# Seven block products of the gated experts: first differences and a second block kept in PSUM, two products of the next unit drawn ahead, weight sums split later

## The chip, the cores and the metric

One core of a Trainium2 chip runs the whole program. The metric is the device time in microseconds (us), median of three runs. TensorE (PE in the profile, PEld its weight loads), VectorE (DVE), ScalarE (ACT), GpSimd (POOL) and the DMA queues work side by side, each in its own program order, and wait for each other through semaphores. SP only issues DMAs.

## The reference, cut to what matters

Attention with a bias, then a dense layer with softplus, then eight experts whose outputs are weighted by a gate that is normalised over tokens and experts. The change lies in the last part alone:

```
N, D, E, F = (1152, 512, 8, 1024)
P = np.exp(logits)            # then 8 rounds of row and column normalisation
for e in range(E):
    h = np.maximum(x @ w1[e], 0.0)
    ye = h @ w2[e]
    out += P[:, e:e + 1] * ye
```

Everything is fp32. Each operand of a matmul is split into a high part (rounded) and a low part (the rest), and a product is three matmuls: high by high, low weights by high, high weights by low.

## The kernel before, in words

**Units.** The two feed-forward stages are cut into 40 units of 256 hidden columns: units 0 to 7 are the dense layer, and each expert has four. Units 12 to 39 (experts 1 to 7) are "gated": their hidden values are multiplied by the gate `pb` right after the ReLU. Units 12 to 38 are "fast" and are the subject here. Of 1152 tokens, 1024 go through blocked products and the last 128 through plain ones (`up_last`, `turn_last`, `last_sum`).

**Seven products in place of eight.** Tokens and hidden columns are split in two by two blocks, and both matrix products of a unit are done with seven block products (Strassen, Winograd's form) instead of eight. In the text P1 to P7 are the up products (x by w1, six matmuls each, 128x512 out), and D1 to D7 the down products (h by w2, six matmuls each). The blocks of h are B11, B12, B21, B22; their sums are T1 = B12 - B11, T2 = B22 - T1, T3 = B22 - B12, T4 = B21 - T2. D1 takes B11, D5 takes T1, D6 takes T2, D3 B22, D7 T3, D2 B21, D4 T4. "First" of a block is ACT's rounded copy (high part), "second" the subtraction that gives the low part, on DVE or POOL.

**PSUM.** Chains `X`, `Y`, `Z` are running sums: P1, P6, P7, P4 add into bank `t`, P2 sits in `tail`, P5 and P3 in `pv`. The four `sum` banks take the down products.

**Order of a fast unit on PE before.** P2, P6, P5, P7, P3, the plain product of the last tokens (in bank `tail`), P4, then P1 of the next unit, then D1, two transposes, D5, D6, `last_sum`, D3, D7, D2, D4. `after` runs what follows each product: copies of the running sum to SBUF on ACT (`keep`: v1 after P1, u2 after P6, u3 after P5), and for P2, P7, P3, P4 an addition (`add`) and `weighted`, one DVE instruction max(x, 0) * pb that gives B22, B11, B12, B21, followed by the differences and splits. Before, B11 and T1 are in SBUF: `u3` and a half of `fs[2]`.

**Weights.** `load` brings w1 into `fs[0]` and w2 into `fs[3]` by SP's DMAs. `mix` (POOL, four instructions) writes the sums of the w1 blocks to `fs[1]`, `mixd` (POOL, four) those of w2 to `fs[4]`. `high` and `highd` split w1 (`wu`) and w2 (`wd`), `highs` the sums in `fs[4]` (tiles `raw` for the high part, `room` for the low part). In gated units a split by `parts` is two ACT instructions of 128x1024, high = src and low = -src, and a DMA issued by POOL that adds src to low. `DOWN_JOBS` says after which down product of a unit each of these is issued.

**Entry.** At unit 12 the gate's columns come from DRAM (`shares_of(1)` for `pb`, `publish` for expert 0), and the sum of expert 0 so far is multiplied by them (`weigh_columns`).

Of the kernel before, what the change touches and what calls it, by code (L numbers as in the profile page):

```python
# [11 lines left out]
F32R = mybir.dt.float32r  # L12
# [101 lines left out]
def attention_moe_moe_kernel(ctx: ExitStack, tc, qT, kT, vN, wpos, w_in, w_out, w_gate, e_w1, e_w2,  # L114
# [503 lines left out]
    def experts(m0, accp, xr):  # L618
# [107 lines left out]

        def parts(w, src, by_dma=False):
            hi, lo = (w[:, 0], w[:, 1]) if not isinstance(w, tuple) else w
            nc.scalar.activation(hi, src, AF.Copy)  # L729
# [23 lines left out]
        def highs(u, k):  # L753
            if fast(u):
                if not wss:
                    wss.extend([again(3, [128, 1024], F32R), pool["spare"][:, 0:1024]])
                parts(tuple(wss), fs[4], True)

# [103 lines left out]

        full = {}

        def weighted(u, n, src):
            name = {2: "B22", 7: "B11", 3: "B12", 4: "B21"}[n]
            extra = [fs[2][:, 512 * k:512 * k + 512] for k in range(2)]
            full[name] = hold["u3"] if n == 4 and fast(u) else extra[0] if n == 4 else hold[{2: "v1", 7: "u3", 3: "u2"}[n]]
            c = int(n in (7, 4))
            if fast(u) and n == 3:  # L870
                full.update(T1=extra[0], T2=extra[1], T3=full["B12"])
            elif fast(u) and n == 4:
                full["T4"] = extra[1]
            t = h[name] = pool["moe"].tile([128, 2, 512], F32R, tag="h", bufs=4, name="h")
            nc.vector.scalar_tensor_tensor(out=full[name], in0=src, scalar=0.0, in1=pb[c], op0=ALU.max, op1=ALU.mult)  # L875
            if not fast(u):
                first(name)
                h[c, int(n in (7, 3))] = t
                lows.append(lambda: second(nc.vector, name))
            elif n == 2:  # L880
                held.append(lambda: first(name))
            elif n == 7:
                first(name)
                second(nc.gpsimd, "B22")
            elif n == 3:
# [4 lines left out]
                first("T1")  # L890
                first("T2")
                second(nc.vector, "T1")
                second(nc.gpsimd, "T2")
                difference(nc.gpsimd, "T3", "B22", "B12")
            else:
                h["T4"] = tss[2]
                first(name)

        def soften(u, c, f):
# [50 lines left out]
        def up_last(u):  # L950
            zr, n, xl = bank("t" if u < U1 and u in PLAIN else "tail"), 0, pool["xl"]
            for k in range(KT):
# [15 lines left out]
        def down_fast(u):  # L968
            product(u + 1, 1)
            begun.add((u + 1, 1))  # L970
            banks = {x: ps2("sum") for x in "XZ"}
            for at, (n, x, a, b, (c, i)) in enumerate(DOWN):
# [3 lines left out]
                for k, f in order:  # L976
                    wo, ho = ((0, 0), (1, 0), (0, 1))[k]
                    nc.tensor.matmul(banks[x][:, f], ws[wo][:, o + 128 * f:o + 128 * f + 128], h[b][:, ho],  # L978
                                     start=(n in (1, 5, 2) and k == 0), stop=(k == 2), skip_group_check=True)
                for fs_ in (slice(0, 2),) if at else (slice(0, 1), slice(1, 2)):  # L980
                    d = acc[c][:, 2 * i:2 * i + 2][:, fs_]
                    nc.vector.tensor_tensor(out=d, in0=banks[x][:, fs_], in1=d, op=ALU.add)  # L982
                if at == 0:
                    turn_last(u)
                    difference(nc.gpsimd, "T4", "B21", "T2")
                    first("T3")
                    second(nc.gpsimd, "T3")
                    if u > U1 + UE:
                        weights["high"](u + 1, 1)
                    first("T4")  # L990
                    second(nc.gpsimd, "B21")
                    second(nc.gpsimd, "T4")
                if at == 3:
                    after(u + 1, 1)
                if at == 2:
                    r = last_sum(u, "pv")
                if at == 6:
                    evac(u, 2, 0, r)
                for what, ahead, k in DOWN_JOBS.get(at, ()):
# [5 lines left out]

        def weigh_columns(c, i):
            d = acc[c][:, 2 * i:2 * i + 2]
            nc.vector.tensor_tensor(
                out=d, in0=d, in1=pb["first"][:, 512 * c:512 * c + 512].rearrange("p (o n) -> p o n", o=1).to_broadcast([128, 2, 512]),
                op=ALU.mult)  # L1010
# [203 lines left out]
        def publish():  # L1214
# [112 lines left out]
        def unit(u):  # L1327
# [87 lines left out]
            ask(u, "r2")  # L1415
            if gated(u) and (u + 1 - U1) % UE == 0 and u + 1 < NU:
                shares_of((u + 1 - U1) // UE)
            load_up()
# [212 lines left out]
```

## Time and profile before

| what | value |
|---|---|
| median of 3 runs | 1238.3 us (1238.29 to 1239.51) |
| the profiled execution: its own time, its span | 1237.1 us, 1235.3 us |
| busy of the span: PE, DVE, POOL, ACT | 94%, 77%, 68%, 59% |
| P2 of unit 13 to P2 of unit 14 | 22.77 us |
| P2 of unit 14 to P2 of unit 39, 25 units | 610.73 us |

All times are us from the start of the span. A row of a timeline is: start, duration, engine, line, operation, output and inputs, sizes, how many merged, and in brackets the idle time of the engine before it and what ended that. A row of the windows view is: the stretch, its length, the busy time of PE, PEld, DVE, ACT and POOL with their instructions, the granted TensorE clock as a share of full speed, the busy share of the DMA engines and GB/s. A row of instruction groups ends with the busy time, the mean of one in ns, and the idle time before them.

### The profile page before, as it was taken

How to read it: one execution, taken by the hardware profiler on the slowest of the kernel's cores; microseconds unless marked ns; L12 is line 12 of the kernel's file. 1: busy time of each engine (PE TensorE's matmuls, PEld its weight loads, DVE VectorE, ACT ScalarE, POOL GpSimd, SP SyncE). 2: the span in 40 equal slices, each digit the busy share in tenths (PEclk: the TensorE clock that was granted, in tenths of full speed). 3: DMA queues.
4: the chain of work that ended last, by engine and by line, in shares of the span. 5: the costliest groups of instructions: out<-in, count | busy, mean ns of one | idle time of the engine just before them, and what ended most of it. 6: DMA issues, size and time to landing. Idle time of an engine off the chain costs nothing.

```text
span 1235.3 us, 19730 instructions
## 1 busy us (share of the span) xinstructions
PE 1166.2 (94%) x7289; PEld 959.0 (78%) x7289; DVE 952.2 (77%) x1472; ACT 727.3 (59%) x1190; POOL 835.7 (68%) x854
## 2 busy tenths in 40 slices
PE   5989999999999999989999999999999999999998
PEld 5888999888888878768777777777777777777777
DVE  9976988498888665658778877878777878777874
ACT  7976887775455553345654565566556555654552
POOL 8236777567878853336777777678767876777770
PEclk9999999999999999989999999999999999999999
DMA  5769663033223211074566566655666567557552
GB/s 137 229 172 249 205 199 90 1 104 102 78 94 102 69 34 35 1 182 92 120 138 151 122 137 132 149 121 127 143 136 130 121 144 162 114 121 159 136 103 94
DMA packets 82568, 152.41 MB, mean 123 GB/s; under 512 B 9312, under 2 KB 47016, under 8 KB 82472
## 3 DMA queue, kind: packets, MB, share of 16 engines
q0 software_dynamic: 15984, 58.20, 25.4%
q1 hardware_dynamic: 66056, 92.51, 24.7%
q8 instruction: 57, 0.93, 0.3%
q10 hardware_dynamic: 432, 0.45, 0.1%
q14 instruction: 39, 0.32, 0.1%
HBM read 78.79 MB, written 14.14 MB: 75 GB/s over the span
## 4 chain that ended last, share of the span: by engine, by line
PE 68%; DVE 20%; DMA 4%; ACT 3%; issue 3%; POOL 1%; SPq 1%; DVEq 0%; ACTq 0%; POOLq 0%
PE sum L978 18%; PE t L815 10%; PE sum L1044 10%; DVE u L875 9%; PE pv L815 5%; PE op L544 5%; PE pv L1060 4%; PE tail L815 4%; DVE f L861 3%; PE sps L453 3%; PE tp L503 2%; DVE u L838 2%; PE tail L954 1%; DVE pv L838 1%; PE t L833 1%
## 5 line engine op out<-in xcount | busy, mean ns | idle before, releaser
L982 DVE TENSOR_TENSOR acc<-sum,acc 128x512 f32<-128x512 f32 (+1 forms) x216 | 232.8, 1088 | 68.8 <-PE sum L978 60.1
L815 PE MATMUL t<-room,wu 128*128 128x512 f32 x592 | 161.1, 391 | 1.0 <-ACT u L843 0.5
L858 POOL TENSOR_TENSOR raw<-f,raw 128x512 fp32r<-128x512 f32 x54 | 77.3, 1431 | 124.5 <-ACT raw L854 124.5
L854 ACT ACTIVATE h<-u 128x512 fp32r<-128x512 f32 x83 | 52.5, 633 | 177.7 <-DVE u L875 146.0
L1044 PE MATMUL sum<-h,wd 128*128 128x512 f32 x576 | 138.7, 394 | 0.0
L815 PEld LDWEIGHTS t<-room,wu 128*128 128x128 f32 x592 | 110.3, 188 | 26.1 <-ACT u L843 1.4
L1044 PEld LDWEIGHTS sum<-h,wd 128*128 128x128 f32 x576 | 105.4, 188 | 22.2 <-DVE acc L1081 0.9
L815 PE MATMUL pv<-x,wu 128*128 128x512 f32 x444 | 114.8, 394 | 5.9 <-ACT u L843 5.8
L978 PE MATMUL sum<-h,wd 128*128 128x512 f32 x324 | 93.8, 413 | 26.2 <-DVE h L858 26.0
L729 ACT ACTIVATE wu<-f 128x1024 fp32r<-128x1024 f32 x77 | 81.0, 1052 | 41.1 <-POOL f L725 23.6
L815 PEld LDWEIGHTS pv<-x,wu 128*128 128x128 f32 x444 | 83.8, 190 | 24.3 <-ACT u L843 6.7
L978 PEld LDWEIGHTS sum<-h,wd 128*128 128x128 f32 x324 | 56.8, 188 | 57.1 <-DVE h L858 36.5
L875 DVE SCALAR_TENSOR_TENSOR u<-u,pb 128x512 f32<-128x512 f32 x28 | 91.2, 3256 | 1.0
L815 PE MATMUL t<-x,wu 128*128 128x512 f32 x296 | 85.5, 390 | 0.0
L838 DVE TENSOR_TENSOR u<-t,u 128x512 f32<-128x512 f32 x37 | 25.6, 691 | 75.9 <-PE t L815 73.6
L854 ACT ACTIVATE raw<-f 128x512 fp32r<-128x512 f32 x81 | 50.7, 626 | 55.8 <-DVE f L861 55.2
L269 PE MATMUL pac<-bw,m 128*128 128x64 bf16 (+1 forms) x1920 | 66.8, 198 | 17.3 <-DVE bw L241 12.0
L269 PEld LDWEIGHTS <-m 128*128 128x128 bf16 (+1 forms) x1920 | 63.1, 105 | 20.9 <-issue 9.6
L734 POOL TENSOR_TENSOR wu<-f,wu 128x1024 fp32r<-128x1024 f32 x21 | 53.0, 2523 | 38.1 <-ACT wu L729 37.4
L858 POOL TENSOR_TENSOR h<-u,h 128x512 fp32r<-128x512 f32 x54 | 77.9, 1443 | 0.0
L732 POOL DMA_DIRECT2D wu<-f x56 | 49.6, 886 | 39.8 <-ACT wu L731 23.4
L1081 DVE TENSOR_TENSOR acc<-sum,acc 128x512 f32<-128x512 f32 x80 | 55.1, 688 | 24.7 <-PE sum L1044 24.0
(296 smaller groups left out, 3168.8 us busy)
## 6 DMA issues: line engine op xcount, KB each, us to landing
f<-in_e_w_dram SPq DMA_DIRECT2D x128, 256.0 KB, 4.0
wu<-f POOLq DMA_DIRECT2D x56, 512.0 KB, 4.6
wd<-f POOLq DMA_DIRECT2D x28, 512.0 KB, 6.7
room<-f POOLq DMA_DIRECT2D x27, 512.0 KB, 7.5
raw<-in_w_in_dram SPq DMA_DIRECT2D x16, 512.0 KB, 3.6
raw<-in_w_out_dram SPq DMA_DIRECT2D x16, 512.0 KB, 3.4
bias<-wt SPq DMA_DIRECT2D x14, 576.0 KB, 5.4
raw<-in_qT_dram SPq DMA_DIRECT2D x16, 288.0 KB, 5.4
```

What stands on the lines that cost most here:

```text
L269: nc.tensor.matmul(pt[0:n, g], lhs, win(w, (k * (ng + 1) + gw) * NC, [[(ng - gw) * NC, 2], [1, NC]]), start=(k == 0), stop=(k == 2))
L544: nc.tensor.matmul(op[:, 0:n], l, r, start=(part == 0 and k == 0), stop=(part == 8))
L729: nc.scalar.activation(hi, src, AF.Copy)
L815: nc.tensor.matmul(zz, wu(u)[:, a, o:o + 128], xs[xn][b][j], start=(n in (1, 2, 5) and k == 0), stop=(k == 5), skip_group_check=True)
L838: nc.vector.tensor_tensor(out=out, in0=hold[bank_], in1=hold[name], op=ALU.add)
L854: nc.scalar.activation(h[name][:, 0], full[name], AF.Copy)
L858: eng.tensor_tensor(out=t[:, 1], in0=full[name], in1=t[:, 0].bitcast(F32), op=ALU.subtract)
L875: nc.vector.scalar_tensor_tensor(out=full[name], in0=src, scalar=0.0, in1=pb[c], op0=ALU.max, op1=ALU.mult)
L978: nc.tensor.matmul(banks[x][:, f], ws[wo][:, o + 128 * f:o + 128 * f + 128], h[b][:, ho], start=(n in (1, 5, 2) and k == 0), stop=(k == 2) ...
L982: nc.vector.tensor_tensor(out=d, in0=banks[x][:, fs_], in1=d, op=ALU.add)
L1044: nc.tensor.matmul(s, lhs, rhs, start=(n == 0), stop=(n == 5))
L1081: nc.vector.tensor_tensor(out=d, in0=o, in1=d, op=ALU.add)
```

## The change

Four things in fast units. B11 is written to the PSUM bank that P2 used (`tail`) and T1 to that of P5 and P3 (`pv`); T2 and T4 share one half of `fs[2]`. The plain product of the last tokens goes to the `sum` bank `Z`, and the splits of T1 and T2 and the difference T3 move behind it (`split_t`). B21 is computed after D1 instead of after P4. P2 of the next unit is drawn ahead into the down products, between D7 and D2. The split of the w2 sums moves from the down products (both ACT instructions and the DMA after D2) into the next up products: the high part after P6, the low part with its DMA after P5, and `mix` of the next unit behind it. At the entry, `pb` is loaded before expert 0's columns, these come in two halves to two places, and two of the four multiplications by them go from DVE to POOL.

```diff
-        def parts(w, src, by_dma=False):
+        def parts(w, src, by_dma=False, steps=(0, 1)):
...
         def add(u, bank_, name):
-            out = hold[name if name == "u3" or (u < U1 and name == "v1") else bank_]
+            out = hold["Y" if gated(u) and name == "u3" else name if name == "u3" or (u < U1 and name == "v1") else bank_]
...
-        def weighted(u, n, src):
+        def weighted(u, n, src, ready=False):
+            if n == 4 and fast(u) and not ready:
+                later.append(lambda: weighted(u, n, src, True))
+                return
-            full[name] = hold["u3"] if n == 4 and fast(u) else extra[0] if n == 4 else hold[{2: "v1", 7: "u3", 3: "u2"}[n]]
+            full[name] = hold[{2: "v1", 7: "Y", 3: "u2", 4: "u3"}[n]]
-                full.update(T1=extra[0], T2=extra[1], T3=full["B12"])
+                full.update(T1=hold["Z"], T2=fs[2][:, 0:512], T3=full["B12"])
...
+        def split_t():
+            first("T1")
+            first("T2")
+            second(nc.vector, "T1")
+            second(nc.gpsimd, "T2")
+            difference(nc.gpsimd, "T3", "B22", "B12")
...
-            if n in (6, 4):
+            if n in ((5, 4) if fast(u) else (6, 4)):
                 while held:
                     held.pop(0)()
...
-            zr, n, xl = bank("t" if u < U1 and u in PLAIN else "tail"), 0, pool["xl"]
+            if fast(u):
+                hold["sums"] = {x: ps2("sum") for x in "XZ"}
+            zr, n, xl = hold["sums"]["Z"][:, 0] if fast(u) else bank("t" if u < U1 and u in PLAIN else "tail"), 0, pool["xl"]
...
+                if at == 4:
+                    product(u + 1, 2)
+                    begun.add((u + 1, 2))
...
-            pb["first"] = raws[2]
-            nc.sync.dma_start(out=raws[2].rearrange("p (t n) -> p t n", n=128), in_=shares(0, 0, 8))
             shares_of(1)
+            for c, t in ((0, raws[2][:, 0:512]), (1, fs[2][:, 512:1024])):
+                pb["first", c] = t
+                nc.sync.dma_start(out=t.rearrange("p (t n) -> p t n", n=128), in_=shares(0, 4 * c, 4))
...
-        DOWN_JOBS = {1: (("mixd", 1, 0),), 3: (("high", 2, 0),), 4: (("highd", 1, 0),), 5: (("highs", 1, 0), ("mix", 2, 0))}
+        DOWN_JOBS = {1: (("mixd", 1, 0),), 3: (("high", 2, 0),), 4: (("highd", 1, 0),)}
...
                     if u == U1 + UE and n == 5:
-                        tss.extend(again(k, [128, 2, 512], F32R) for k in range(3))
+                        tss.extend(again(k, [128, 2, 512], F32R) for k in range(2))
+                        for i in range(2):
+                            weigh_columns(nc.gpsimd, 0, 1 - i)
...
+                    if u > U1 + UE and p in (6, 5):
+                        weights["highs"](u, (6 - p,))
+                        if p == 5:
+                            weights["mix"](u + 1, 0)
```

DVE's order between D4 and D5 of a fast unit, before (`u_9176` is u3, `u_9166` u2, `v_9111` v1, `f_4646` `fs[2]`; line 875 is `weighted`, line 861 a difference, 858 a second, 982 the sums of the down products):

```order
L982 TENSOR_TENSOR acc<-sum,acc 128x1024 x6
L1083 SCALAR_TENSOR_TENSOR acc<-pv,prob,acc 128x512
L838 TENSOR_TENSOR tail<-tail,v_9111 128x512
L875 SCALAR_TENSOR_TENSOR v_9111<-tail,pb 128x512
L838 TENSOR_TENSOR u_9176<-t,u_9176 128x512
L875 SCALAR_TENSOR_TENSOR u_9176<-u_9176,pb 128x512
L838 TENSOR_TENSOR pv<-pv,u_9166 128x512
L875 SCALAR_TENSOR_TENSOR u_9166<-pv,pb 128x512
L861 TENSOR_TENSOR f_4646<-u_9166,u_9176 128x512
L858 TENSOR_TENSOR h<-u_9176,h 128x512
L861 TENSOR_TENSOR f_4646<-v_9111,f_4646 128x512
L858 TENSOR_TENSOR raw<-f_4646,raw 128x512
```

The same place now (lines 880, 864, 861, 994 in their place):

```order
L994 TENSOR_TENSOR acc<-sum,acc 128x1024 x2
L841 TENSOR_TENSOR tail<-tail,v_9101 128x512
L880 SCALAR_TENSOR_TENSOR v_9101<-tail,pb 128x512
L841 TENSOR_TENSOR tail<-t,u_9159 128x512
L880 SCALAR_TENSOR_TENSOR tail<-tail,pb 128x512
L841 TENSOR_TENSOR pv<-pv,u_9149 128x512
L880 SCALAR_TENSOR_TENSOR u_9149<-pv,pb 128x512
L864 TENSOR_TENSOR pv<-u_9149,tail 128x512
L861 TENSOR_TENSOR h<-tail,h 128x512
L864 TENSOR_TENSOR f_4646<-v_9101,pv 128x512
L861 TENSOR_TENSOR raw<-pv,raw 128x512
```

The sequence of the steps is the same, but B11 and T1 now have their output, and their readers an input, in the banks `tail` and `pv`.

ACT's order from the copy v1 to the split of B11, before (`f_2601` is `fs[0]`, `f_4647` `fs[3]`, `f_4648` `fs[4]`; lines 729 and 731 are the two instructions of a split, 843 `keep`, 854 a first):

```order
L843 ACTIVATE v_8367<-t 128x512
L729 ACTIVATE wu_2599<-f_2601 128x1024
L731 ACTIVATE wu_2599<-f_2601 128x1024
L729 ACTIVATE wd_4645<-f_4647 128x1024
L731 ACTIVATE wd_4645<-f_4647 128x1024
L729 ACTIVATE raw<-f_4648 128x1024
L731 ACTIVATE room<-f_4648 128x1024
L843 ACTIVATE u_8422<-t 128x512
L854 ACTIVATE h<-v_8367 128x512
L843 ACTIVATE u_8432<-pv 128x512
L854 ACTIVATE h<-u_8432 128x512
```

The same place now (lines 846, 730, 734, 857):

```order
L846 ACTIVATE v_8361<-t 128x512
L730 ACTIVATE wu_2599<-f_2601 128x1024
L734 ACTIVATE wu_2599<-f_2601 128x1024
L730 ACTIVATE wd_4645<-f_4647 128x1024
L734 ACTIVATE wd_4645<-f_4647 128x1024
L846 ACTIVATE u_8409<-t 128x512
L730 ACTIVATE raw<-f_4648 128x1024
L846 ACTIVATE u_8419<-pv 128x512
L857 ACTIVATE h<-v_8361 128x512
L734 ACTIVATE room<-f_4648 128x1024
L857 ACTIVATE h<-tail 128x512
```

The two copies of the w2 sums stand behind u2 and behind the first of B22, where they stood ahead of u2. POOL's order is as before: `mixd`, the three DMAs (wu, wd, room), `mix`, the second of B22.

## Rows read from the trace of the kernel before

**Rows 1.** Windows: unit 12, unit 13, and units 14 to 38
```profile
541.21:571.36 30.15, 24.30 (x105) 19.39 (x104) 20.41 (x23) 13.79 (x21) 12.85 (x13) 0.89 0.38 98
571.36:594.13 22.77, 22.68 (x106) 18.27 (x104) 17.79 (x22) 13.90 (x20) 16.99 (x18) 1.00 0.64 139
594.13:1204.86 610.73, 576.29 (x2602) 454.90 (x2601) 484.75 (x526) 346.16 (x498) 462.60 (x474) 1.00 0.62 134
```

**Rows 2.** PE's waits from 594 to 1204: total, times, longest
```profile
PE sum L978 <- DVE h L858: 26.0, 24, 1.3
PE tail L963 <- ACT gl L958: 8.1, 24, 0.3
```

**Rows 3.** PE's timeline: P7, P3, D1 and transposes of one unit; unit 12's D1
```profile
1013.91 1.52 PE L815 MATMUL t<-room,wu 128*128 128x512 f32 x6
1015.27 1.52 PE L815 MATMUL pv<-x,wu 128*128 128x512 f32 x6
...
1020.81 0.61 PE L978 MATMUL sum<-h,wd 128*128 128x512 f32 x2
1022.49 1.19 PE L978 MATMUL sum<-h,wd 128*128 128x512 f32 x4 [1.06 <-DVE h L858]
1024.02 0.44 PE L963 MATMUL tail<-ident,gl 128*128 128x128 f32 x2 [0.34 <-ACT gl L958]
...
559.85 1.53 PE L978 MATMUL sum<-h,wd 128*128 128x512 f32 x6
561.22 0.38 PE L963 MATMUL tail<-ident,gl 128*128 128x128 f32 x2
```

**Rows 4.** DVE's timeline: the sum of P7 and B11 of the same unit; unit 39's B11
```profile
1015.57 0.69 DVE L838 TENSOR_TENSOR u<-t,u 128x512 f32<-128x512 f32 x1 [2.26 <-PE t L815]
1016.29 3.48 DVE L875 SCALAR_TENSOR_TENSOR u<-u,pb 128x512 f32<-128x512 f32 x1
...
1212.09 0.69 DVE L875 SCALAR_TENSOR_TENSOR u<-u,pb 128x512 f32<-128x512 f32 x1
```

**Rows 5.** Instruction groups by form, 600 to 1200
```profile
L875 DVE SCALAR_TENSOR_TENSOR u<-u,pb 128x512 f32<-128x512 f32 x25 | 86.8, 3473 | 0.8
...
L875 DVE SCALAR_TENSOR_TENSOR u<-pv,pb 128x512 f32<-128x512 f32 x25 | 17.3, 691 | 0.9
...
L858 DVE TENSOR_TENSOR h<-u,h 128x512 fp32r<-128x512 f32 x25 | 17.1, 682 | 0.0
...
L729 ACT ACTIVATE raw<-f 128x1024 fp32r<-128x1024 f32 x24 | 25.5, 1062 | 34.6 <-POOL f L751 34.4
...
L843 ACT ACTIVATE u<-pv 128x512 f32<-128x512 f32 x24 | 14.2, 591 | 0.1
```

**Rows 6.** POOL's timeline beside that B11: first and last of five in a row
```profile
1014.30 1.61 POOL L722 TENSOR_TENSOR f<-f 128x512 f32<-128x512 f32 x1
...
1017.64 1.57 POOL L858 TENSOR_TENSOR h<-v,h 128x512 fp32r<-128x512 f32 x1
```

**Rows 7.** The page's slices: busy tenths of POOL, 30.9 us each
```profile
POOL 8236777567878853336777777678767876777770
```

**Rows 8.** Tiles wu, wd and room, 600 to 1200: landing of POOL's DMAs, in that order
```profile
DMA to landing us min/median/max: 4.5/4.6/6.0
...
DMA to landing us min/median/max: 6.6/6.7/8.1
...
DMA to landing us min/median/max: 6.9/7.5/10.0
```

**Rows 9.** Timelines of the entry: B22 on DVE, P3 on PE; landing of pb
```profile
548.88 0.69 DVE L875 SCALAR_TENSOR_TENSOR v<-tail,pb 128x512 f32<-128x512 f32 x1 [5.35 <-DMA pb<-pt]
...
552.66 2.92 PE L815 MATMUL pv<-x,wu 128*128 128x512 f32 x6 [5.85 <-ACT u L843]
...
DMA to landing us min/median/max: 10.9/11.9/12.9
```

**Rows 10.** The page's groups: POOL's two-input instruction of 128x1024
```profile
L734 POOL TENSOR_TENSOR wu<-f,wu 128x1024 fp32r<-128x1024 f32 x21 | 53.0, 2523 | 38.1 <-ACT wu L729 37.4
```

More of the change, by code (lines that the diff above doesn't have):

```diff
@@ L725, in mix @@
             nc.gpsimd.tensor_tensor(out=at(t, 128), in0=at(t, 0), in1=at(t, 128), op=ALU.subtract)
-        def parts(w, src, by_dma=False):
+        def parts(w, src, by_dma=False, steps=(0, 1)):
             hi, lo = (w[:, 0], w[:, 1]) if not isinstance(w, tuple) else w
-            nc.scalar.activation(hi, src, AF.Copy)
+            if 0 in steps:
+                nc.scalar.activation(hi, src, AF.Copy)
+            if 1 not in steps:
+                return
             if by_dma:
@@ L861, in difference @@
             eng.tensor_tensor(out=full[out], in0=full[a], in1=full[b], op=ALU.subtract)
-        full = {}
-        def weighted(u, n, src):
+        full, later = {}, []
+        def weighted(u, n, src, ready=False):
+            if n == 4 and fast(u) and not ready:
+                later.append(lambda: weighted(u, n, src, True))
+                return
             name = {2: "B22", 7: "B11", 3: "B12", 4: "B21"}[n]
-            extra = [fs[2][:, 512 * k:512 * k + 512] for k in range(2)]
-            full[name] = hold["u3"] if n == 4 and fast(u) else extra[0] if n == 4 else hold[{2: "v1", 7: "u3", 3: "u2"}[n]]
+            full[name] = hold[{2: "v1", 7: "Y", 3: "u2", 4: "u3"}[n]]
             c = int(n in (7, 4))
             if fast(u) and n == 3:
-                full.update(T1=extra[0], T2=extra[1], T3=full["B12"])
+                full.update(T1=hold["Z"], T2=fs[2][:, 0:512], T3=full["B12"])
             elif fast(u) and n == 4:
-                full["T4"] = extra[1]
+                full["T4"] = full["T2"]
             t = h[name] = pool["moe"].tile([128, 2, 512], F32R, tag="h", bufs=4, name="h")
@@ L889, in weighted @@
                 difference(nc.vector, "T2", "B22", "T1")
[L890 to L894, printed above, removed]
             else:
-                h["T4"] = tss[2]
                 first(name)
+        def split_t():
[4 more added lines that the diff above has]
+            difference(nc.gpsimd, "T3", "B22", "B12")
         def soften(u, c, f):
@@ L958, in up_last @@
             nc.scalar.activation(gl, zr[:, 0:256], AF.Softplus if u < U1 else AF.Relu)
+            if fast(u):
+                split_t()
         def turn_last(u):
@@ L970, in down_fast @@
             begun.add((u + 1, 1))
-            banks = {x: ps2("sum") for x in "XZ"}
+            banks = hold["sums"]
             for at, (n, x, a, b, (c, i)) in enumerate(DOWN):
@@ L979, in down_fast @@
                                      start=(n in (1, 5, 2) and k == 0), stop=(k == 2), skip_group_check=True)
+                if u == U1 + UE and at in (0, 6):
+                    weigh_columns(nc.vector, c, i)
                 for fs_ in (slice(0, 2),) if at else (slice(0, 1), slice(1, 2)):
@@ L984, in down_fast @@
                     turn_last(u)
+                    later.pop()()
+                    if (u + 1 - U1) % UE == 0:
+                        shares_of((u + 1 - U1) // UE)
                     difference(nc.gpsimd, "T4", "B21", "T2")
@@ L989, in down_fast @@
                         weights["high"](u + 1, 1)
+                    second(nc.gpsimd, "B21")
+                if at == (2 if u == U1 + UE else 0):
+                    if len(tss) < 3:
+                        tss.append(again(2, [128, 2, 512], F32R))
+                    h["T4"] = tss[2]
                     first("T4")
-                    second(nc.gpsimd, "B21")
                     second(nc.gpsimd, "T4")
@@ L996, in down_fast @@
                     r = last_sum(u, "pv")
+                if at == 4:
+                    product(u + 1, 2)
+                    begun.add((u + 1, 2))
+                if at == 4:
+                    evac(u, 2, 0, r)
                 if at == 6:
-                    evac(u, 2, 0, r)
+                    after(u + 1, 2)
                 for what, ahead, k in DOWN_JOBS.get(at, ()):
@@ L1004, in again, with weigh_columns @@
             return (m0 if n < 2 else pool["moe"]).tile(shape, dtype, tag=f"raw{n}", bufs=1, name="raw")
-        def weigh_columns(c, i):
+        def weigh_columns(eng, c, i):
             d = acc[c][:, 2 * i:2 * i + 2]
-            nc.vector.tensor_tensor(
-                out=d, in0=d, in1=pb["first"][:, 512 * c:512 * c + 512].rearrange("p (o n) -> p o n", o=1).to_broadcast([128, 2, 512]),
+            eng.tensor_tensor(
+                out=d, in0=d, in1=pb["first", c].rearrange("p (o n) -> p o n", o=1).to_broadcast([128, 2, 512]),
                 op=ALU.mult)
@@ L1415, in unit @@
             ask(u, "r2")
-            if gated(u) and (u + 1 - U1) % UE == 0 and u + 1 < NU:
-                shares_of((u + 1 - U1) // UE)
             load_up()
```

4 lines of the change are left out of this document (1 added, 3 removed).

## The prediction

> **What bounds the kernel now.** I read the windows first, then what PE waited for, then one unit's timeline on PE, DVE and POOL. The fast units take half of the run: 25 of them take 610.73 us, 24.43 each, while unit 13 takes 22.77 with PE busy for 22.68 of it [rows 1]. So PE is nearly the bound, and something takes 1.7 us from each unit but this one. The waits name it: the down product's matmul waits for a DVE subtraction in 24 units, 26.0 us in all, and the transposes wait for ACT's `gl`, 8.1 us [rows 2]. The reader is to see in the timeline that both stand at one place: D1 issues two matmuls at 1020.81 and its third, which needs the low part of B11, at 1022.49; the transposes come at 1024.02 [rows 3].
>
> Followed back from there, P7 starts at 1013.91 and its sum on DVE at 1015.57, so a product is usable 1.66 us after its start [rows 3, 4]. B11 starts at 1016.29 and takes 3.48 us, 3.47 on average over 25 units, where the same instruction with a PSUM input takes 0.69 [rows 4, 5]. What stretches it is POOL. It runs five instructions back to back from 1014.30 to 1019.21, and B11 ends 0.56 us after the last of them [rows 4, 6]. In unit 39, where POOL's slice shows no busy tenth, the same form takes 0.69 [rows 4, 7]. And 0.7 us earlier the sum of P7, with a PSUM and an SBUF input, took its normal 0.69 beside POOL's instruction of 1.61 [rows 4, 6]. I conclude that a DVE instruction with two SBUF inputs stands still while POOL has work, and one with a PSUM input does not.
>
> **The change part by part.** *B11 and T1 in PSUM.* After this no DVE instruction of a steady unit has two SBUF inputs. What D1 loses now: six matmuls take 1.37 us where nothing waits (559.85 to 561.22), 0.23 each, so the third would stand at 1020.81 + 0.46 = 1021.27 and stands at 1022.49: 1.22 us. The four that follow would bring the transposes to 1022.49 + 0.92 = 1023.41, and they stand at 1024.02: 0.61 us [rows 3]. Together 1.83 us; 24.43 - 1.83 = 22.60, which agrees with unit 13's 22.77 from below.
>
> What is late next: P7 no longer sets the end, P3 does. From P3's start its sum begins at 1.66; the sum, B12, T1 and the second of B11 take 0.69, 0.69, 0.69 and 0.68, with small gaps 4.5 in all [rows 4, 5]. D1's third matmul stands 5.54 + 0.46 = 6.0 behind P3 [rows 3]. That leaves 1.5 us of cover. The durations from PSUM are taken from B12 (691 ns), which reads PSUM already, against 682 for a subtraction in SBUF [rows 5].
>
> *The plain product in bank `Z`, T1 and T2 split behind it.* `gl` now comes ahead of the two firsts on ACT, so the transposes no longer wait for those; this is the 0.61 above. D5 starts 5.54 + 1.37 + 0.2 = 7.1 after P3; T2's difference ends at 5.2, the first of T1 about 0.6 later. Cost nothing, hidden by D1.
>
> *P2 drawn ahead, B21 later.* PE's instructions are the same in number; P2 between D7 and D2 gives T4's low part 1.36 us more. Nothing on the path; I count 0.
>
> *The w2 sums split later.* ACT's high copy (1.06 us) now stands between u2 and u3. From P5's start, u2 starts at 0.3 and ends at 0.9, the copy ends at 2.0, u3 (0.59) at 2.5; P3, which needs u3, starts at 2.72 [rows 3, 5]. It fits by 0.2 us, and whatever the copy is late comes out of PE. It waited for `mixd` before, 34.4 us in 24 units, 1.4 each [rows 5], when it stood ahead of u2; as it now stands some 2 us later in the unit, I count no wait. The low copy ends at about 4.2 (the first of B22, 0.63, is ahead of it), and POOL issues the DMA at 4.3. D5's third matmul needs its result at 1.36 + 6.90 + 1.37 + 0.2 + 0.46 = 10.3 [rows 3]. So 6.0 us are left to a transfer that lands after 7.5 in the median, 6.9 to 10.0 [rows 8]. But this figure is that of the third in a row of three: the first (wu) lands after 4.6, the second (wd) after 6.7 [rows 8]; the steps look like a queue. Now wd is issued some 4 us ahead of room, so I take 4.6, the row of a transfer that is first in the queue, and keep 7.5 and 10.0 for the rivals. Queued behind POOL's DMA are `mix`, the second of B22 and that of T2; they come later than before, but T2's low part is needed only late in D6. No cost.
>
> So 25 units gain 1.83 each: 45.8 us.
>
> *The entry.* Unit 12 takes 30.15 us, 7.38 more than unit 13, at a granted clock of 0.89 [rows 1]. DVE's B22 waits 5.35 us for `pb`; ACT's first of it stands ahead of u3, and so P3 waits 5.85 us [rows 9]. Now `pb` goes ahead of the columns, and u3 ahead of the first of B22, so this chain no longer reaches PE. In its place: ACT's two copies into wu (1.06 each) still stand ahead of u3, which makes P3 0.8 us late. And DVE's multiplication of expert 0's second half has two SBUF inputs, while POOL does the first half in two instructions of 2.5 us each [rows 10] and then T2's and T3's. As B11 did, it would wait until POOL pauses, about 2.3 us past the point where the last-token sum needs DVE. I take 7.4 - 3.1 = 4.3. The bounds are 7.4, and nothing or 2 us worse, if `pb` still lands after the 10.9 to 12.9 us that it needs now [rows 9] and DVE's wait comes on top.
>
> Here a rule of the Trainium skill is worth weighing. The row shows that B11, started at 1016.29, waited not for one POOL instruction but also for one that began at 1017.64, after it [rows 4, 6]. "SBUF — State Buffer", section "SBUF: two separate sides", says that GpSimd and a DVE instruction with two SBUF inputs share a port pair, which whoever starts first holds for one whole instruction. By that rule DVE would get its turn between POOL's instructions, the 2.3 us would go, and the total would be 1186. I go by the row.
>
> The sum: 45.8 + 4.3 = 50.1. The profiled execution took 1237.1 us, 1.2 less than the median of 1238.3; 1237.1 - 50.1 = 1187.0, and against the median 1188.
>
> **Rivals.** *The sums' low part lands late.* If the DMA lands after more than 6.0 us, D5 waits for the rest in every unit. At 7.5 that is 1.5 of the 1.83 us: 25 x 0.33 + 4.3 = 12.6, or 1226; at 6.5 it is 1201. For it: the median of 7.5, and the loads of `fs` that start at the same time. Against it: the steps of [rows 8].
>
> *The same, and slower than before.* At the largest landing seen, 10.0, D5 waits 4.0 us: units of 26.6, 25 x 2.17 - 4.3 = 50 us more, 1288. This decides against the change from a landing of 6.0 + 1.83 = 7.8 us on. Against it: 10.0 was a single maximum.
>
> *B11 stays slow.* The change would not do what it says if B11's 3.48 us came from something other than its two SBUF inputs, say from `pb`. Then D1 goes on waiting, and only the transposes' 0.61 and the entry go: 25 x 0.61 + 4.3 = 19.6, 1219. For it: no row shows this very form with a PSUM input beside four POOL instructions. Against it: the sum of P7 beside POOL, and unit 39.
>
> **How the numbers follow.** Forecast 0.72, with a range of its own of 1180 to 1200 (entry between nothing and 7.4, units between 22.5 and 22.8). Low part late but faster 0.12, with 1200 to 1232. B11 slow 0.06. Slower 0.05. Some 0.05 for a new wait that eats most of the gain, of which 0.02 ends within 0.2% (2.5 us, about what a measurement of this kernel can tell from no change). So faster 0.93, same 0.02, slower 0.05. The range of 1180 to 1216 holds the forecast's and the nearer half of the first rival.
>
> **What would show it.** In the profile of the changed kernel `weighted` of B11 should take 0.69 us, D1 and the transposes should have no idle time ahead of them, P2 to P2 should be 22.6 us, and unit 12 some 26. D5 waiting for a DMA of `room`, or P3 for ACT's u3, would prove the cover of the later split wrong; a B11 of 3 us would prove the mechanism wrong.

## The result and the profile after

The changed kernel takes 1184.1 us (1182.52 to 1186.91) against 1238.66 us (1238.29 to 1239.51) before (medians of four runs each): ratio 0.9561, 95% interval 0.9542 to 0.958. 1188 was forecast, in a range of 1180 to 1216. The profiled executions took 1182.52 us (span 1180.7) and 1237.1 us (span 1235.3), so 54.6 us of span have to be found.

The windows view of the kernel after, for unit 12, unit 13 and units 14 to 38 (P2 to P2; P2 of a unit now stands 2.72 us earlier, in the down products of the unit before):

```profile
541.80:563.24 21.44, 19.96 (x94) 16.10 (x92) 14.26 (x18) 11.03 (x18) 15.02 (x11) 1.00 0.54 139
563.24:586.24 23.00, 22.42 (x105) 18.42 (x104) 17.91 (x23) 13.78 (x21) 17.47 (x19) 1.00 0.55 121
586.24:1145.94 559.70, 557.77 (x2602) 459.94 (x2601) 415.06 (x526) 345.23 (x500) 460.84 (x476) 1.00 0.68 146
```

25 units take 559.70 us, 22.39 each, where they took 610.73 [rows 1]: 51.0 us gained. PE is busy for 557.77 us of them, so it is the bound now. Unit 12, from P6 to P6 of unit 13, takes 24.17 us (543.16 to 567.33) against 30.15 (542.57 to 572.72): 6.0 gained. From P2 of unit 39 to the end it takes 34.76 us, which with P2 2.72 earlier is 1.6 more than the 30.44 before, and unit 12 begins 0.6 later. Unit 13 takes 0.2 more from P6 to P6 (22.99 against 22.77): 51.0 + 6.0 - 1.6 - 0.6 - 0.2 = 54.6.

PE's waits after, from 560 to 1160:

```profile
PE t L818 <- DMA wu<-f: 1.6, 2, 1.2
PE t L818 <- ACT u L846: 1.2, 1, 1.2
PE sum L988 <- DMA room<-f: 0.9, 3, 0.6
```

The 26.0 us before D1's third matmul and the 8.1 before the transposes [rows 2] are gone. The wait for `u` is one, in unit 39. PE's, DVE's and POOL's timelines after, of one unit: P7, P3, D1, the transposes and D5; then the sum of P7, B11, T1 and the second of B11; then the start of POOL's row:

```profile
593.04 1.52 PE L818 MATMUL t<-room,wu 128*128 128x512 f32 x6
594.40 1.52 PE L818 MATMUL pv<-x,wu 128*128 128x512 f32 x6
...
599.94 1.53 PE L988 MATMUL sum<-h,wd 128*128 128x512 f32 x6
601.31 0.38 PE L973 MATMUL tail<-ident,gl 128*128 128x128 f32 x2
601.45 0.71 PE L988 MATMUL sum<-raw 128*128 128x512 f32 x2
```

```profile
594.66 0.70 DVE L841 TENSOR_TENSOR tail<-t,u 128x512 f32<-128x512 f32 x1 [1.51 <-PE t L818]
595.39 0.70 DVE L880 SCALAR_TENSOR_TENSOR tail<-tail,pb 128x512 f32<-128x512 f32 x1
...
597.59 0.70 DVE L864 TENSOR_TENSOR pv<-u,tail 128x512 f32<-128x512 f32 x1
598.20 0.68 DVE L861 TENSOR_TENSOR h<-tail,h 128x512 fp32r<-128x512 f32 x1
```

```profile
596.54 1.61 POOL L722 TENSOR_TENSOR f<-f 128x512 f32<-128x512 f32 x1
```

B11 takes 0.70 us where it took 3.48 [rows 4]. But POOL's row is no longer beside it: with the w2 sums split later, the row begins at 596.54, and B11 ends at 596.09. What runs beside that row now is T1 and the second of B11, each with one input in PSUM, at 0.70 and 0.68 us. So this profile alone doesn't tell whether PSUM or POOL's later row freed B11; numbers 2 and 3 below do. D1 runs its six matmuls in one piece. The second of B11 ends at 598.88, D1's third matmul stands at 599.94 + 0.46 = 600.40: the cover of 1.5 us behind P3 is there. ACT's timeline of this unit (u2, the high copy of the w2 sums, u3, the low copy), POOL's issue of the DMA for it, and the landing of `room` from 600 to 1150:

```profile
591.94 0.60 ACT L846 ACTIVATE u<-t 128x512 f32<-128x512 f32 x1 [3.21 <-PE t L818]
592.44 1.05 ACT L730 ACTIVATE raw<-f 128x1024 fp32r<-128x1024 f32 x1
593.39 0.59 ACT L846 ACTIVATE u<-pv 128x512 f32<-128x512 f32 x1
...
594.38 1.06 ACT L734 ACTIVATE room<-f 128x1024 fp32r<-128x1024 f32 x1
```

```profile
595.97 0.85 POOL L735 DMA_DIRECT2D room<-f  x1 [3.67 <-issue]
```

```profile
DMA to landing us min/median/max: 5.0/5.4/6.3
```

u3 ends at 593.98, 0.42 us ahead of P3. The DMA, issued at 595.97, lands after 5.4 us and not after 7.5 [rows 8], at about 601.4; D5's third matmul wants it at 601.99. The cover is 0.6 us, and 3 units missed it.

### The profile page after: what moved, and what is told of

Same layout as the page of the kernel before. It is cut to its first block, busy times and chain, and to the rows that moved or that the text cites. A ratio compares the mean times of both kernels' runs of the same rounds, so it can differ in the third digit from the quotient of the medians.

```text
span 1180.7 us, 19762 instructions
## 1 busy us (share of the span) xinstructions
PE 1143.6 (97%) x7289; PEld 960.9 (81%) x7289; DVE 878.8 (74%) x1470; ACT 724.7 (61%) x1190; POOL 840.1 (71%) x856
## 4 chain that ended last, share of the span: by engine, by line
PE 82%; DVE 7%; DMA 5%; issue 2%; ACT 2%; POOL 1%; SPq 1%; DVEq 0%; ACTq 0%; POOLq 0%
PE sum L988 20%; PE t L818 15%; PE sum L1068 10%; PE pv L818 7%; PE op L544 5%; PE pv L1084 4%; PE tail L818 4%; PE sps L453 3%; PE sum L962 3%; PE tp L503 2%; DMA room<-f 2%; PE t L836 1%; PE tail L962 1%; DMA wu<-f 1%; DMA bias<-wt 1%
## 5 line engine op out<-in xcount | busy, mean ns | idle before, releaser
L1068 PE MATMUL sum<-h,wd 128*128 128x512 f32 x576 | 138.8, 395 | 0.0
L1068 PEld LDWEIGHTS sum<-h,wd 128*128 128x128 f32 x576 | 105.4, 188 | 22.3 <-DVE acc L1105 0.9
L735 POOL DMA_DIRECT2D room<-f x27 | 23.1, 855 | 88.3 <-issue 86.6
L861 POOL TENSOR_TENSOR raw<-f,raw 128x512 fp32r<-128x512 f32 x54 | 85.4, 1582 | 0.0
L988 PE MATMUL sum<-h,wd 128*128 128x512 f32 x324 | 82.3, 389 | 0.0
L988 PEld LDWEIGHTS sum<-h,wd 128*128 128x128 f32 x324 | 60.8, 188 | 12.6
L846 ACT ACTIVATE u<-t 128x512 f32<-128x512 f32 x37 | 22.1, 599 | 79.5 <-PE t L818 79.5
L988 PE MATMUL sum<-raw 128*128 128x512 f32 x216 | 67.4, 410 | 1.1 <-DVE acc L994 1.1
L818 PEld LDWEIGHTS t<-x,wu 128*128 128x128 f32 x296 | 55.4, 188 | 13.2 <-DMA wu<-f 2.9
```

Of the source, the lines that this page charges most:

```text
L818: nc.tensor.matmul(zz, wu(u)[:, a, o:o + 128], xs[xn][b][j], start=(n in (1, 2, 5) and k == 0), stop=(k == 5), skip_group_check=True)
L861: eng.tensor_tensor(out=t[:, 1], in0=full[name], in1=t[:, 0].bitcast(F32), op=ALU.subtract)
L1068: nc.tensor.matmul(s, lhs, rhs, start=(n == 0), stop=(n == 5))
```

## The experiments

Each kernel is the changed one with the edit shown, unless another is named. "Unit" is the mean from P2 of unit 14 to P2 of unit 39, over 25. Each ratio is to the kernel before as it ran beside that kernel (medians of 1238.65 to 1239.35 us).

| kernel | time, us | ratio to before | unit, us |
|---|---|---|---|
| before | 1238.66 | | 24.43 |
| changed | 1184.1 | 0.9561 [0.9542, 0.958] | 22.39 |
| changed again | 1183.77 (1183.15 to 1191.56) | 0.9577 [0.9553, 0.9601] | 22.45 |
| 1, P2 not ahead | 1191.22 | 0.9619 [0.9598, 0.964] | 22.65 |
| 2, B11 in SBUF | 1274.15 | 1.0282 [1.0262, 1.0303] | 25.71 |
| 3, before with B11 in PSUM | 1191.3 | 0.9614 [0.9598, 0.9631] | 22.56 |
| 4, sums split early | 1204.64 | 0.9721 [0.9692, 0.9749] | 23.14 |
| 5, neither | 1203.11 | 0.9703 [0.9687, 0.972] | 23.13 |
| 6, B11 in SBUF, no `mix` | 1191.3 | 0.9613 [0.9593, 0.9632] | 22.46 |
| 7, last unit and entry | 1190.23 | 0.9606 [0.9591, 0.962] | 22.52 |
| 8, columns first | 1192.27 | 0.962 [0.9606, 0.9635] | 22.57 |
| 9, last unit only | 1185.08 | 0.9573 [0.9554, 0.9592] | 22.45 |
| 10, B11 in SBUF, a gap | 1217.1 | 0.9827 [0.9809, 0.9845] | 23.64 |
| 12, columns ahead, last unit | 1187.07 | 0.9571 [0.9555, 0.9588] | 22.56 |

**1, P2 not drawn ahead.**

```diff
-                if at == 4:
-                    product(u + 1, 2)
-                    begun.add((u + 1, 2))
...
-                if at == 6:
-                    after(u + 1, 2)
```

> The changed kernel, with P2 of the next unit put back behind D4. My prediction counted its place at 0 us. In the trace of the changed kernel a steady unit takes 22.25 us where I forecast 22.60, and the weight loads of the kernel before waited 9.5 us in 25 units for DVE's sums of the down products, which is 0.38 a unit. If P2's place between D7 and D2 gives DVE the time for the sums of D3 and D7, units take 22.5 to 22.6 us without it and the kernel 1191 to 1194 us. If the place is worth nothing, as predicted, units stay at 22.25 and the kernel at 1184.

Measured: 1191.22 us, units of 22.65. (The 22.25 of the expectation is a unit in which nothing waits; the mean over 25 is 22.39.) So P2's place is worth 22.65 - 22.39 = 0.26 us a unit, 6.5 in all; the prediction counted nothing. This holds with the later split of the sums: with the early one, numbers 4 and 5 below, the unit is 23.14 with P2 ahead and 23.13 without. The weight loads' waits from 594 to 1146, of the kernel before and of this one:

```profile
PEld sum L978 <- DVE acc L982: 8.4, 22, 0.4
```

```profile
PEld sum L988 <- DVE acc L994: 9.1, 24, 0.4
```

In the changed kernel no such row is left: P2 between D7 and D2 gives DVE the time of one product to add up the banks that D2 and D4 want. The row stood in the trace before, but in none of the rows on which the prediction goes.

**2, B11 in SBUF again; 3, the kernel before with B11 and the plain product in PSUM and nothing else; 6, as 2 without POOL's `mix`.**

```diff
-            out = hold["Y" if gated(u) and name == "u3" else name if name == "u3" or (u < U1 and name == "v1") else bank_]
+            out = hold[name if name == "u3" or (u < U1 and name == "v1") else bank_]
...
-            full[name] = hold[{2: "v1", 7: "Y", 3: "u2", 4: "u3"}[n]]
+            full[name] = hold[{2: "v1", 7: "u3", 3: "u2", 4: "u3"}[n]]
```

> The changed kernel, with B11 back in SBUF (u3) and everything else as changed. B11's own instruction now starts about 1 us before POOL's mix and should take 0.69 us; but T1 (u2 and u3) and the second of B11 have two SBUF inputs again and start while POOL runs mix and the second of B22, from 596.5 to 601.5 in the unit whose P6 is at 590.3. If such an instruction waits until POOL pauses, T1 starts at about 601.4 and not 597.6, D1 waits 2.3 us in every unit, units take 24.6 us and the kernel about 1244. If it waits for one POOL instruction at a time, T1 and the second lose about 1.3 us each, D1's cover of 1.5 to 2 us holds nearly all of it and the kernel takes 1184 to 1200. If the two inputs have nothing to do with it, 1184.

> The kernel before, with one part of the change alone: B11 in the PSUM bank of P2, and, since that bank is then taken, the plain product of the last tokens in the sum bank Z. T1, B21, P2, the splits of the sums and the entry stay as before. My theory: B11 takes 0.69 us, D1 and the transposes lose their 1.83 us, units take 22.6 to 22.75 and the kernel 1193 to 1197 us. The rival, that the gain needs the splits behind the plain product or the later split of the sums too, gives units of 23.5 us or more and 1215 or more.

> B11 in SBUF (u3), as in the run with 1274 us, and POOL's mix left out in units 13 to 38: the sums of w1's blocks are not made anew, so up products use old ones (the output is not the reference's). In that run T1, the one DVE instruction with two SBUF inputs that then starts beside POOL, took 4.56 us. Theory: it waits for POOL's instructions. Without the four of mix only the second of B22 may stand beside it: T1 0.7 to 1.9 us, within the cover of 1.5 us before D1, units of 22.4 to 22.8, 1184 to 1196. Rival: two SBUF inputs are slow there for another reason (DMA traffic, the place in the unit): T1 stays at 4.5 us and the time at 1265 to 1275.

Number 3 alone gains 24.43 - 22.56 = 1.87 us a unit, 46.8 in all, a little more than its forecast. Of the 54.6 us by the medians it has 47.4; all other parts together bring 7. In it POOL's row still stands beside B11. B11, and the POOL instruction that runs over its whole length:

```profile
984.65 0.70 DVE L875 SCALAR_TENSOR_TENSOR tail<-tail,pb 128x512 f32<-128x512 f32 x1
```

```profile
984.55 1.03 POOL L725 TENSOR_TENSOR f<-f 128x256 f32<-128x256 f32 x1
```

It takes 0.70 us in all 25 units, and in numbers 4 and 5, where the row also stands beside it, as well. That is the row which the rival "B11 stays slow" asked for, and the rival fell. Number 2 is slower than before, and than any theory had it. Here B11 comes before POOL's row and takes its 0.7, with two SBUF inputs; it is T1, which now also has two, that stands still. T1's output lies in PSUM in the changed kernel too; only its input B11 differs. DVE's and POOL's timelines of number 2:

```profile
1017.90 4.51 DVE L864 TENSOR_TENSOR pv<-u,u 128x512 f32<-128x512 f32 x1
```

```profile
1016.39 0.85 POOL L735 DMA_DIRECT2D room<-f  x1 [3.94 <-issue]
1016.95 1.61 POOL L722 TENSOR_TENSOR f<-f 128x512 f32<-128x512 f32 x1
1018.20 1.05 POOL L723 TENSOR_TENSOR f<-f 128x256 f32<-128x256 f32 x1
...
1020.30 1.54 POOL L861 TENSOR_TENSOR h<-v,h 128x512 fp32r<-128x512 f32 x1
```

T1 ends at 1022.41, 0.57 after POOL's fifth instruction (1021.84): as far as B11 ended behind POOL before. The unit's extra 3.32 us are 83 in all: PE waits 57.7 us for DVE (53.3 for T1's followers, 4.4 for sums), and its own busy time grows by 27 us, from 557.8 to 585.1, at a granted clock of 0.97. That clock was missing from the expectation. Number 6 takes four of POOL's five instructions away, and T1 falls from 4.56 to 1.28 us on average, the unit to 22.46. So it is POOL's work that held it. The rival, slow for another reason, fell.

**4, the w2 sums split in the down products as before; 5, that and P2 not ahead.**

```diff
-        DOWN_JOBS = {1: (("mixd", 1, 0),), 3: (("high", 2, 0),), 4: (("highd", 1, 0),)}
+        DOWN_JOBS = {1: (("mixd", 1, 0),), 3: (("high", 2, 0),), 4: (("highd", 1, 0),), 5: (("highs", 1, 0), ("mix", 2, 0))}
...
-                    if u > U1 + UE and p in (6, 5):
-                        weights["highs"](u, (6 - p,))
-                        if p == 5:
-                            weights["mix"](u + 1, 0)
```

> The changed kernel, with the w2 sums split in the down products as before (both ACT instructions and the DMA after D2, mix of the next unit behind them). Theory: POOL's mixd now ends about 0.3 us after P6 starts, so the two ACT instructions end 2.3 us after it and u2 at 2.9, where P7 needs it at 2.72: PE waits 0.2 to 0.3 us a unit, and the kernel takes 1188 to 1193. The rival, that the later split is worth nothing or costs what little PE waits for room (0.9 us in all), gives 1183 to 1184.

> The changed kernel with P2 not drawn ahead and the w2 sums split in the down products as before; B11 and T1 in PSUM, plain product in bank Z, entry of the change stay. Alone, taking P2's place back cost 7 us (1191.2) and taking the later split back cost 20 us (1204.6). Theory A, the two are one edit: without P2 ahead, P6 comes 1.36 us later behind D7, so ACT's copies of the w2 sums are done before u2 is due and P7 doesn't wait; units of 22.6 us as in before with B11 in PSUM, 1190 to 1193. Rival, each has its price by itself: 1184 + 7 + 20 = 1211.

All theories missed, in both: 1204.64 and 1203.11. Splitting the sums later is worth 0.75 us a unit with P2 ahead (23.14 to 22.39) and 0.48 without (23.13 to 22.65). ACT's and PE's timelines of number 4 show how it is lost:

```profile
991.33 1.06 ACT L730 ACTIVATE raw<-f 128x1024 fp32r<-128x1024 f32 x1 [1.88 <-POOL f L754]
992.29 1.04 ACT L734 ACTIVATE room<-f 128x1024 fp32r<-128x1024 f32 x1
993.24 0.58 ACT L846 ACTIVATE u<-t 128x512 f32<-128x512 f32 x1
```

```profile
993.87 1.66 PE L818 MATMUL t<-room,wu 128*128 128x512 f32 x6 [0.58 <-ACT u L846]
```

The copies wait for POOL's `mixd`, u2 stands behind them, and P7 waits for u2. In number 3 the same copies stand ahead of u2 too and nothing is lost. The difference is `mixd`, read against D1 of the unit, which starts at 966.72 in number 3 and at 973.66 in number 5. POOL's `mixd` in number 3; then, in number 5, the difference T4 on POOL and `mixd`:

```profile
975.55 1.71 POOL L751 TENSOR_TENSOR f<-f 128x256 f32<-128x256 f32 x2
```

```profile
977.59 1.31 POOL L864 TENSOR_TENSOR f<-u,f 128x512 f32<-128x512 f32 x1 [0.62 <-DVE u L880]
...
983.96 1.71 POOL L754 TENSOR_TENSOR f<-f 128x256 f32<-128x256 f32 x2
```

`mixd` starts 8.83 us behind D1 in the one, 10.30 in the other: POOL's row of differences and seconds ahead of it ends 1.5 us later. Two moves have a share in this. POOL's second of T2 starts 0.28 us behind D1 in number 3 and 0.76 in number 5, since T1 and T2 are split behind the plain product: 0.5 us. T4 then waits 0.62 us for DVE's B21, and the DMA of wu waits 0.3 longer for ACT's copies, which stand behind the first of B21: 1.0 us with B21 after D1. The shares are read from these rows; no kernel changed either move by itself. So the later split of the sums is what makes the two moves free.

**8, the columns of expert 0 loaded ahead of `pb`, as before.**

```diff
-            shares_of(1)
             for c, t in ((0, raws[2][:, 0:512]), (1, fs[2][:, 512:1024])):
...
+            shares_of(1)
```

> The changed kernel with the columns for expert 0 loaded ahead of pb again, as before; nothing else differs. Theory A (the prediction's): the entry gains because pb lands earlier; then pb lands 4.9 us later, at about 548.9, and since DVE's B22 stands ahead of the sum of P7 and of B11, D1's third matmul is late by 0 to 1.5 us: 1184 to 1186. Theory B: what counts is that ACT's copy u3 no longer stands behind the first of B22; pb's place is hidden, PE's wait at P3 stays 0.4 us and the time is the changed kernel's, 1184. Rival: pb's place is all of it, 6 us lost, 1190.

Measured 1192.27 us, some 8 slower: more than the theories A and B had, and nearest to the rival's 1190, though not by its mechanism alone. DVE's timeline at the entry: B22 and B11.

```profile
548.38 0.69 DVE L880 SCALAR_TENSOR_TENSOR v<-tail,pb 128x512 f32<-128x512 f32 x1 [4.86 <-DMA pb<-pt]
...
551.96 0.70 DVE L880 SCALAR_TENSOR_TENSOR tail<-tail,pb 128x512 f32<-128x512 f32 x1 [2.06 <-DMA pb<-pt]
```

`pb` comes late in both halves, and D1's third matmul waits 1.29 us. P3 waits the same 0.41 us as in the changed kernel, so u3's place ahead of the first of B22 does hide the late B22. So A was right on D1 and B on P3. Unit 12 is 5.6 us longer (27.03 against 21.44, P2 to P2). D1's waits are 1.6 of it (0.36 for ACT's first of B11, then the 1.29). D6's wait is another 1.7: 2.8 us in place of 1.1, which is the next subject. The last 2.2 are PE's own time, 22.18 us against 19.96: after D6's wait TensorE ran at the lower of its two levels, 1.2 GHz (the next two matmuls took 1.19 us for 0.70), and the granted clock of unit 12 is 0.94 in place of 1.00. Against number 9, in which `pb` comes first and D6 waits 3.2 us, unit 12 is only 1.8 longer, so the price of `pb`'s place lies between 1.8 and 5.6. The units after it are 0.18 us longer on average. Half of that is one unit, 26.13 us against 23.83, in which PE waits 1.95 us for a DMA of wu where it waited 1.24; the rest I can't explain.

**7, two copies moved on ACT; 9, one of them; 11, the changed kernel again.** In 7 and 9 the first of B22 stands behind u2 and u3 in unit 39 as it does in fast units; in 7 also the second pair of copies into `wu` stands behind u3 in unit 12.

```diff
+                if n == 2:
+                    held.append(split)
...
-            if n in ((5, 4) if fast(u) else (6, 4)):
+            if n in ((5, 4) if gated(u) else (6, 4)):
...
-                    if n == 3 and u == U1 + UE:
+                    if n == 4 and u == U1 + UE:
                         weights["high"](u + 1, 1)
```

> The changed kernel with two copies moved on ACT: in unit 39 the first of B22 stands behind u2 and u3 (where P7 waits 1.21 us for u2), and in unit 12 the second pair of copies into wu behind u3 (where P3 waits 0.41 us). If these waits are on the path that sets the end: 1.6 us less than the changed kernel, 1182.5. Rival: other waits take their place (in unit 39 the plain product waits for the second of B11, in unit 12 D6 for the sum of D1): 1184.

> The changed kernel with the first of B22 behind u2 and u3 in unit 39 alone; the entry stays as in the change. The run with both moves lost 5 us in unit 12 and gained 1.1 us from P2 of unit 39 to the end (33.65 against 34.76 us). Theory: the gain at the end stands by itself: 1.1 us less than the changed kernel in this call, about 1183. Rival: the lower end comes from another timing of the output's DMAs and the time is the changed kernel's.

> The changed kernel once more, beside the others of this call: 1182.5 to 1187, and in unit 12 either the short wait for DVE's multiplication of expert 0 (1.1 us, the profile so far) or the long one (2.8 to 5.7, as in the profiles of six variants), with P2 of unit 12 to P2 of unit 13 at 21.4 or at 24 to 27 us.

P7's wait in unit 39 goes, and the end gets 1.1 us shorter in both (from P2 of unit 39, 33.65 and 33.7 us against 34.76). But number 7 loses 5.6 us in unit 12, P2 to P2, where the 0.41 us of P3 were to be had, and number 9, unchanged there, loses 3.75 (2.15 by D6's wait, 3.2 us, and 1.6 by PE's own time, at a granted clock of 0.93). Their total is the changed kernel's (9) or more (7). In 7, PE's waits from 535 to 575 and the window of unit 12:

```profile
PE sum L995 <- DVE acc L1001: 5.7, 1, 5.7
```

```profile
542.16:569.20 27.04, 21.38 (x93) 17.51 (x92) 17.82 (x18) 12.81 (x20) 15.58 (x13) 0.87 0.50 110
```

D6 waits 5.7 us for the sum of D1, and after it TensorE runs at its lower level for a while (D6's next two matmuls take 1.19 us for 0.70): the granted clock of the stretch is 0.87, where the changed kernel has 1.00. DVE's sum stands behind its multiplication of expert 0's second half, which has two SBUF inputs. In the changed kernel (DVE, then POOL):

```profile
554.19 1.95 DVE L1032 TENSOR_TENSOR acc<-acc,f 128x1024 f32<-128x1024 f32 x1
```

```profile
550.30 4.76 POOL L1032 TENSOR_TENSOR acc<-acc,raw 128x1024 f32<-128x1024 f32 x2 [0.31 <-DMA raw<-pt]
555.02 2.27 POOL L861 TENSOR_TENSOR raw<-f,raw 128x512 fp32r<-128x512 f32 x1
```

and in number 9, whose order of instructions is the same here:

```profile
553.18 4.09 DVE L1039 TENSOR_TENSOR acc<-acc,f 128x1024 f32<-128x1024 f32 x1
```

```profile
547.38 1.61 POOL L861 TENSOR_TENSOR h<-v,h 128x512 fp32r<-128x512 f32 x1
548.64 5.08 POOL L1039 TENSOR_TENSOR acc<-acc,raw 128x1024 f32<-128x1024 f32 x2
...
554.62 1.57 POOL L864 TENSOR_TENSOR u<-v,u 128x512 f32<-128x512 f32 x1
```

In the first DVE gets its turn between two POOL instructions, and the next of POOL takes 2.27 us, since it waits in turn. In the second DVE waits until POOL has ended its row, at 556.2, and ends at 557.27. What differs on POOL is 0.31 us in which it waited for the columns' DMA. Number 11 had 0.49 there and 2.13 us for the multiplication. In every profile with POOL's two multiplications, a POOL that had stood idle within its row before the contested place let DVE in (1.5 to 2.4 us, numbers 2, 6, 8, 10, 11, 12 and the changed kernel); one that had run without a gap since its DMA issue did not (4.08 to 5.45 us, numbers 1, 4, 5, 7 and 9).

**10, as 2, with a gap in POOL's row:** the first of B22 behind that of B11 on ACT, and `mix` behind the second of B22.

```diff
             elif n == 7:
                 first(name)
+                held.pop(0)()
                 second(nc.gpsimd, "B22")
...
-            if n in ((5, 4) if fast(u) else (6, 4)):
+            if n in ((4,) if fast(u) else (6, 4)):
...
-                        if p == 5:
-                            weights["mix"](u + 1, 0)
+                    if u > U1 + UE and p == 7:
+                        weights["mix"](u + 1, 0)
```

> B11 in SBUF as in the run with 1274 us, so that T1 has two SBUF inputs; the first of B22 moves behind that of B11 on ACT, so that POOL waits for it between its DMA issue and the second of B22, with mix behind that. POOL does the same work beside T1, but after an idle gap. Theory 1, POOL holds until it pauses: T1 waits for the second of B22 and all of mix, 5 to 6.5 us, units of 26.5 to 28, 1290 to 1320. Theory 2, from the multiplications in unit 12: POOL keeps DVE out from instruction to instruction only in a row that follows its DMA issue without a gap (its instructions then overlap in the records, 1.6 us for one that comes every 1.25); after a gap DVE gets in behind one instruction: T1 1.3 to 2.0 us, units of 22.4 to 23, 1186 to 1205.

DVE's and POOL's timelines: T1 and the second of B11; POOL from its DMA issue on.

```profile
1002.45 1.75 DVE L864 TENSOR_TENSOR pv<-u,u 128x512 f32<-128x512 f32 x1
1004.11 1.78 DVE L861 TENSOR_TENSOR h<-u,h 128x512 fp32r<-128x512 f32 x1
```

```profile
1000.41 0.85 POOL L735 DMA_DIRECT2D room<-f  x1 [2.54 <-DVE u L841]
1002.35 1.29 POOL L861 TENSOR_TENSOR h<-v,h 128x512 fp32r<-128x512 f32 x1 [1.08 <-ACT h L857]
1003.60 1.74 POOL L722 TENSOR_TENSOR f<-f 128x512 f32<-128x512 f32 x1
```

T1 takes 1.75 us beside the same five POOL instructions that held it for 4.51, though `mix` here stands behind the second of B22 and not ahead of it: theory 2 is right on the mechanism, theory 1 fell. For the gap and against this other order as the cause speaks the entry, where number 9 and the changed kernel have the same order. Its time was missed (1217 for 1186 to 1205), because the second of B11 has two SBUF inputs as well and waits behind one instruction of its own, 1.78 us. The two waits of 1.1 us exceed the cover of 1.5; PE waits 0.4 us a unit for this second and 0.4 for the sums behind it, and the unit is 1.25 longer.

**12, POOL's two multiplications of expert 0 ahead of the second of B22, with the edit of number 9.**

```diff
+                    if u == U1 + UE and n == 4:
                         for i in range(2):
                             weigh_columns(nc.gpsimd, 0, 1 - i)
```

> The changed kernel with the first of B22 behind u2 and u3 in unit 39, and in unit 12 POOL's two multiplications of expert 0 put ahead of the second of B22, so that POOL waits for the columns' DMA (landing at about 550) between its DMA issue and this row. Theory, from the run with the gap: after this wait DVE gets in behind one POOL instruction each time, its multiplication takes 1.2 to 3.0 us (a POOL instruction of 128x1024 is 2.4), D6 waits at most 2 us, P2 of unit 12 to P2 of unit 13 is 21.4 to 22.5 and not 24 to 27; with 1.1 us less at the end 1181 to 1184, less scatter than the changed kernel's 1182.5 to 1191.6. Rival: DVE is kept out until POOL pauses as in most profiles, 1186 to 1189.

DVE's multiplication took 2.41 us, as the theory had it. But the columns landed at 553.8, POOL began there, and D6 waited 1.7 and 2.0 us for DVE and POOL: 1187.07. No version tried is faster than the changed kernel by more than the scatter.

## Why the prediction was right, and where it was not

*B11 and T1 in PSUM, `gl` ahead of the firsts: right.* 45.8 us were predicted; number 1, which has all but P2's place, shows 25 x (24.43 - 22.65) = 44.5, and number 3, which has this part almost alone, 46.8. Units of 22.60 were right for this part. That the later split of the sums also moves POOL's row clear of B11 the prediction did not say; number 3 shows that the gain doesn't need it.

*P2 ahead, counted at 0: mis-sized.* It is 6.5 us in the 25 units. The term missed was the wait of D2's weight loads for DVE's sums.

*The later split, counted at 0: right as a cost, for an incomplete reason.* u3 fits (0.42 us in place of 0.2). The landing was taken as 4.6 and is 5.4, so the slack is 0.6 us and not 1.4; the rival that decided at 7.8 did not come. What the prediction did not see is that with B21 after D1, and T1 and T2 split later, the split of the sums had to move: left where it was, it costs 12 us (number 5 against 1) to 20.5 (4 against the changed kernel).

*The entry, 4.3 predicted and 6.0 measured.* The chain was right: P3 no longer waits for `pb`, and u3 is 0.41 us late in place of 0.8. The multiplication on DVE was to cost 2.3 us and cost 1.07 (D6's wait): 7.38 - 0.41 - 1.07 = 5.9. The 7.38 was P3's wait of 5.85 and some 1.5 us of PE's own time at the granted clock of 0.89; both went.

That the second cost came out small is luck. In this profile and in number 11's D6 waits 1.1 and 1.3 us. In numbers 1, 4, 5 and 9, whose entry is the same up to there, it waits 3.2 us, and unit 12 gains 1.1 to 2.6 us from P6 to P6 and not 6.0. In those four DVE waited until POOL's row ended, as the forecast had it from the row of B11; here it had its turn between two POOL instructions. The Trainium skill ("SBUF — State Buffer", section "SBUF: two separate sides") has it that the port pair is held for one whole instruction. That fits this profile, against the row of B11 by which I went, and not those four. Neither holds throughout: the rows of numbers 2 and 10 show one DVE instruction kept out for a whole POOL row or for one instruction, by whether POOL had a gap. The price stays a matter of a DMA's arrival, which may be why the changed kernel's executions spread from 1182.5 to 1191.6; the profiles show only one execution each.

*The last unit: not seen.* B22 there now follows the sums of D2 and D4 on DVE, its first stands ahead of u2 on ACT, and P7 waits 1.21 us for u2 where it waited 0.50. Taking that wait away gave 1.1 of the 1.6 us back at the end (numbers 7 and 9), and number 1, with P2 of unit 39 not ahead, lacks the wait and loses 0.6 there: so 1.0 us of P2's gain is paid back in this unit. The rest I can't name, but for 0.4 us in numbers 7 and 9 in which the plain product waits for the second of B11.

## What to carry to other kernels

A DVE instruction with two SBUF inputs beside a busy POOL cost 2.5 to 6.5 times its 0.70 us here (1.75 and 4.51); giving one operand a PSUM bank that is free anyway took it off that path. The next instruction to stand beside POOL's row needs the same: in number 2 it was T1. When one move in an order makes a later step late, look for the move that pays for it before pricing each alone: here the later B21 and the later split of T1 and T2 belong together with that of the sums. Where PE is nearly full, read the weight loads' waits as well as the matmuls'.

## What the runs showed of the hardware

POOL kept DVE's two-input instruction out over several of its own instructions (4.51 us over five) when these followed its DMA issue without a gap; the records then overlap, 1.6 us for one that comes every 1.25. After an idle time, 0.31 us at the entry of the changed kernel and 1.08 in number 10, the records hardly overlap (1.29 us for one that comes every 1.25), and DVE waited for one instruction. A DVE instruction with one input in PSUM took 0.70 us beside the same row. That the overlap is the cause and not a companion was not tested.
